# Transposes of normalised tokens and attention output moved from TensorE to DMA, first and last attention unit in two parts, another set of planner constants

## The chip, the cores and the metric

The kernel runs on one core of one Trainium2 chip. The metric is device time in microseconds (us) of one execution; the median of the runs is given. Engines are called PE (TensorE, matmul), DVE (VectorE), ACT (ScalarE), POOL (GpSimd) and SP (SyncE, which here only issues DMAs).

## What is computed

Two transformer layers on one sequence of 2048 tokens with 512 channels, 32 heads of 16 channels each and a gated FFN of width 1792:

```python
def _A_ref(x, wqkv, wo):
    qkv = ...                                  # x @ wqkv, split in q, k, v by head
    scores = jnp.einsum("bhqd,bhkd->bhqk", q, k) * (Dh ** -0.5)
    p = _softmax(scores, axis=-1)
    o = jnp.einsum("bhqk,bhkd->bhqd", p, v)
    return (o as tokens x channels) @ wo
def _B_ref(x, w_gate, w_up, w_down):
    return (_gelu(x @ w_gate) * (x @ w_up)) @ w_down
x = x + _A_ref(_layernorm(x), A_wqkv, A_wo)
x = x + _B_ref(_layernorm(x), B_w_gate, B_w_up, B_w_down)
x = x + _A_ref(_layernorm(x), A_wqkv, A_wo)
x = x + _B_ref(_layernorm(x), B_w_gate, B_w_up, B_w_down)
```

Inputs and output are bfloat16. Both layers use the same weights.

## The kernel before

**Units.** The queries of a layer are cut into blocks (`layer_blocks`: four of 512 tokens in the first layer; three of 512 and two of 256 in the second). A block times a group of four heads is a *unit*; there are 72, and units are worked on in this order. Four heads lie at partitions 0, 32, 64 and 96 of a `QT` or `KT` tile, so that a score matmul uses 32 rows of the PE array.

**Two passes over the scores.** The softmax needs the maximum of a row first. In pass 1 (`p1_emit`) PE makes a 128x512 block of scores, queries on the partitions, in one of PSUM banks 0 to 3 (L1507), and DVE reduces one or two banks to row maxima `PM` (L1522). `fin` reduces the maxima of a unit (L897), transposes them (L899), and four small DMAs on SP put the negated maxima into spare rows of the unit's `QT` slot (`negmax`, L916). In pass 2 (`p2_emit`, `p2_tile`) PE makes the scores again, keys on the partitions, with the maximum subtracted in the same matmul, in banks 4 to 6 (L1378); ACT exponentiates one or two banks to `PT`, a part of the tile `SCR` (L1354); PE multiplies by the values `VP` (L1402) into bank 7, where 17 columns per head hold 16 channels and the row sum. `nrm` takes bank 7 to `ACCS` (L948, ACT), makes the reciprocal of the sums on POOL (L966) and the product on POOL (L971), which goes to `ATT`, tokens on the partitions.

**Folds.** A pair of score blocks can be reduced another way: POOL makes the difference of two key blocks, `KD` (L1149); PE makes scores of the difference (L1327); ACT writes the positive part of them to `SCR` (L1334); DVE adds the other block's scores from PSUM and takes the maximum in one instruction (L1517). This is one ACT instruction more and one DVE reduction less. `want_fold` decides when.

**Around attention.** `ln_to_xnt` normalises tokens (statistics on DVE, the rest on POOL, result `XN`, two slots) and turns each 128x512 tile with `transpose_tile` to `XNT`, channels on the partitions: four PE transposes into a bank (L749) and one eviction on ACT or DVE (L668, L666). From `XNT` come K, Q and V (`kproj`, `qproj`, `vproj`; K and Q go through `SG` and a DMA on SP, L811 and L853, to their head's partitions). `outproj` turns `ATT` in the same manner to `ATTT` (two slots), multiplies by `WO` and adds to the residual `X`. `ffn` normalises `X` again, runs 14 gate GEMMs with GELU on ACT (during which no pass 2 runs, since ACT's table is changed), 14 up GEMMs with the product, and the down GEMM.

**The split.** The first three units of the second layer (`split`, `NSPL=3`) are done in two parts: pass 2 runs over three quarters of the keys with the maximum of those (`fin_part`), the partial result is kept in `ATT` (`keep_part`), and after the last quarter of the keys is there the final maximum is found (`fin_rest`), the last quarter goes through pass 2, and `nrm` scales the kept part by the exponential of the difference of the maxima and adds it.

**The order.** Nothing of the order is decided on the chip. While the program is built, a loop at the end of `_build` keeps an estimated clock for each engine and each tile, and emits at each step the instruction that seems best: a pass 1 matmul, a pass 2 matmul, a piece of a GEMM, or a filler matmul on zeros (L1544) when PE's planned load is low. Work around attention consists of generators (chains) that say what they wait for and carry a due time, counted in pairs of pass 1 matmuls. Moves on SP are emitted when their inputs are estimated to be ready. 19 constants steer the choice; `PLAN` gives a row of them for each 16 pairs of pass 1 (`STRETCH`). They say, among other things, how far pass 2 may fall behind pass 1 (LAG), when evictions go to DVE (LAGT), how late a GEMM piece may make the score matmuls (LIM, OV) and when folds are made (FL, GL, FX). Engines then run their queues in order, with semaphore waits made from the tiles' reads and writes.

The emitted order follows from the estimates alone, for instance those of a DMA on SP, with 0.63 us of queue per issue:

```python
if grp is not None:
    clk[eng] = start + T_DMA * nd
    done = max(clk["dma"], clk[eng] + 1.6) + dur
```

## Time and profile before

| | us |
|---|---|
| median of 3 runs | 2549.27 (2549.22 to 2549.44) |
| the profiled execution, its own time | 2550.05 |
| its span, first to last instruction | 2548.3 |
| POOL busy in the span | 589.6 |
| DMA queue of the program, share of 16 engines | 2.8% |
| granted TensorE clock, mean | 0.999 |

The span is cut by the work in it: up to about 26 us inputs arrive and the first tokens are normalised and projected; up to 80 us pass 1 of the first unit runs beside the projections, and no exponential has run yet; from there to 2493 us pass 1 and pass 2 run side by side, with the output projections, the FFN blocks and (around 1290 to 1400 us) the turn of the layers among them; then the last exponentials follow, and from 2516 us the last block's output projection and FFN.

In the profile a line of a group reads: source line, engine, operation, what it writes and reads, partitions x elements and types, count; busy time in us and mean duration of one in ns; idle time of the engine just before, and what ended it. [...]

### The profile page before, as it was taken

The numbers are of one execution on the slowest core, as the hardware profiler recorded it, in microseconds if no ns is written. First come the engines' busy times: TensorE is split into PE (matmuls) and PEld (weight loads), VectorE is DVE, ScalarE is ACT, GpSimd is POOL, SyncE is SP. The second block draws the span as 40 slices with busy tenths as digits, with TensorE's granted clock in tenths as the row PEclk, the third lists the DMA queues.
The fourth block names the chain that finished last, engine by engine and source line by source line (L and its number), as shares of the span: only waits on it lengthen the run. The fifth ranks groups of instructions, "written<-read, shape, count | busy, mean of one in ns | idle before, by whom it ended". The sixth has DMA issues, their size and how long they took to land.

```text
span 2548.3 us, 67924 instructions
## 1 busy us (share of the span) xinstructions
PE 2450.2 (96%) x29939; PEld 1166.4 (46%) x29939; DVE 2423.5 (95%) x3191; ACT 2356.9 (92%) x3111; POOL 589.6 (23%) x722
## 2 busy tenths in 40 slices
PE   7999999999999999999999999999999999999998
PEld 3444443444434454444434455444543445544555
DVE  7999999999999999999998999999999999999993
ACT  7899998999989999999979899999998999989996
POOL 4010123311133213421133211241113211341200
PEclk9999999999999999999999999999999999999999
DMA  3110000000000000000000000000000000000000
GB/s 100 38 56 6 4 8 2 4 2 2 8 2 4 4 2 6 4 2 16 10 5 4 12 2 4 8 4 8 5 8 1 6 6 3 4 3 12 3 7 6
DMA packets 27367, 25.04 MB, mean 10 GB/s; under 512 B 9408, under 2 KB 26048, under 8 KB 27072
## 3 DMA queue, kind: packets, MB, share of 16 engines
q1 hardware_dynamic: 27072, 20.71, 2.8%
q8 instruction: 234, 3.83, 0.6%
q14 instruction: 61, 0.50, 0.1%
HBM read 9.70 MB, written 2.10 MB: 5 GB/s over the span
## 4 chain that ended last, share of the span: by engine, by line
PE 43%; ACT 32%; DVE 23%; issue 1%; POOL 0%; POOLq 0%; ACTq 0%
ACT SCR L1354 29%; DVE PM L1522 22%; PE PS L1507 14%; PE PS L651 12%; PE PS L1402 9%; PE PS L1378 4%; PE PS L1544 4%; ACT SCR L1334 1%; DVE SCR L1517 1%; PE PS L1327 1%; PE PS L749 0%; ACT XNT L668 0%; ACT SG L668 0%; ACT AO L984 0%; ACT ACCS L948 0%
## 5 line engine op out<-in xcount | busy, mean ns | idle before, releaser
L1522 DVE TENSOR_REDUCE PM<-PS 128x1 f32<-128x512 f32 (+1 forms) x2492 | 2207.6, 948 | 56.2 <-PE PS L1378 27.8
L1354 ACT ACTIVATE SCR<-PS 128x1024 bf16<-128x1024 f32 (+1 forms) x2385 | 2002.7, 931 | 72.4 <-PE PS L1378 51.2
L1507 PE MATMUL PS<-KT,QT 32*128 32x512 bf16 x3914 | 1008.2, 384 | 40.0 <-DVE PM L1522 25.2
L1378 PE MATMUL PS<-QT,KT 32*128 32x512 bf16 (+1 forms) x4608 | 926.3, 360 | 14.0 <-ACT SCR L1354 11.9
L1402 PE MATMUL PS<-VP,SCR 128*128 128x51 bf16 (+1 forms) x16384 | 808.9, 187 | 18.2 <-ACT SCR L1354 13.3
L1402 PEld LDWEIGHTS PS<-VP,SCR 128*128 128x128 bf16 x16384 | 571.0, 96 | 509.7 <-issue 427.1
L1507 PEld LDWEIGHTS PS<-KT,QT 32*128 32x128 bf16 x3914 | 240.8, 91 | 514.7 <-DVE PM L1522 298.2
L1544 PE MATMUL PS<-WV,ZER 128*128 128x240 bf16 x2483 | 432.3, 266 | 4.1 <-ACT SCR L1354 4.1
L966 POOL TENSOR_TENSOR RL<-ACCS,CM 128x16 f32<-128x16 f32 (+1 forms) x63 | 173.4, 2753 | 1032.8 <-ACT ACCS L948 1032.5
L1378 PEld LDWEIGHTS PS<-QT,KT 32*128 32x128 bf16 x4608 | 228.9, 91 | 85.7 <-ACT SCR L1354 62.5
L1544 PEld LDWEIGHTS PS<-WV,ZER 128*128 128x128 bf16 x2483 | 189.0, 96 | 67.9 <-issue 53.9
L1112 POOL TENSOR_TENSOR HT<-HT,AO 128x512 bf16<-128x512 bf16 (+1 forms) x109 | 121.2, 1113 | 273.7 <-ACT AO L1110 273.7
L651 PE MATMUL PS<-WD,HT 128*128 128x512 bf16 x448 | 130.6, 381 | 0.1
L651 PE MATMUL PS<-XNT,WU 128*128 128x512 bf16 (+1 forms) x504 | 127.6, 357 | 0.0
L1517 DVE CUSTOM_DVE_ANT_0 SCR<-PS,SCR 128x512 bf16<-128x512 f32 x182 | 118.0, 685 | 6.0 <-PE PS L1507 2.3
L1149 POOL TENSOR_TENSOR KD<-KT 128x512 bf16<-128x512 bf16 x71 | 81.9, 1154 | 176.1 <-PE PS L1327 162.2
L651 PE MATMUL PS<-XNT,WG 128*128 128x512 bf16 (+1 forms) x504 | 119.4, 359 | 1.3 <-ACT HT L1091 0.9
L1091 ACT ACTIVATE HT<-PS 128x512 bf16<-128x512 f32 (+1 forms) x126 | 69.1, 550 | 50.5 <-PE PS L651 49.5
L1334 ACT ACTIVATE SCR<-PS 128x1024 bf16<-128x1024 f32 (+1 forms) x116 | 99.3, 856 | 16.1 <-PE PS L1327 15.6
L986 POOL TENSOR_TENSOR X<-X,AO 128x512 f32<-128x512 f32 x46 | 58.3, 1268 | 197.2 <-ACT AO L984 197.0
L1110 ACT ACTIVATE AO<-PS 128x512 f32<-128x512 f32 (+1 forms) x109 | 63.8, 585 | 0.4
L651 PEld LDWEIGHTS PS<-XNT,WG 128*128 128x128 bf16 x504 | 39.2, 98 | 53.5 <-issue 29.3
(99 smaller groups left out, 884.9 us busy)
## 6 DMA issues: line engine op xcount, KB each, us to landing
KT<-SG SPq DMA_DIRECT2D x64, 64.0 KB
QT<-MT SPq DMA_DIRECT2D x236, 1.0 KB
QT<-SG SPq DMA_DIRECT2D x56, 64.0 KB
out_dram<-AO SPq DMA_DIRECT2D x16, 128.0 KB, 1.7
WG<-in_B_w_gate_dram SPq DMA_DIRECT2D x4, 448.0 KB, 5.1
WU<-in_B_w_up_dram SPq DMA_DIRECT2D x4, 448.0 KB, 4.8
WD<-in_B_w_down_dram SPq DMA_DIRECT2D x4, 384.0 KB, 4.9
SCR<-in_A_x_dram SPq DMA_DIRECT2D x2, 512.0 KB, 5.4
```

The costliest lines, as they stand in the source:

```text
L651: ins = e.matmul(out_ap, lhsT=l, rhs=r_, start=(i == 0), stop=(i == n - 1))
L966: emit("pool", lambda e: e.tensor_tensor(RL[:, s, 0:4 * nq], lsum, CM1[:, 0:4 * nq], op=ALU.pow), r=[("ACCS", s), ("CM1",)], w=[("RL", s)] ...
L1112: emit("pool", lambda e, ft=ft, o=o: e.tensor_tensor(HT[:, ft, 0:n], HT[:, ft, 0:n], AO[:, o, 0:n], op=ALU.mult), r=[("AO", o), ("HT", ft) ...
L1149: emit("pool", lambda e: e.tensor_tensor(KD[:, s, :], KT[:, g, ka * 512:(ka + 1) * 512], KT[:, g, kb * 512:(kb + 1) * 512], op=ALU.subtrac ...
L1334: emit("act", lambda e: e.activation(PT[:, s0:s0 + cnt, :], PS[:, bk:bk + cnt, :], ACTF.Relu), r=bks, w=[("PT", s0 + d) for d in range(cnt ...
L1354: emit("act", lambda e: e.activation(dst, src, ACTF.Exp, scale=DH ** -0.5), r=[BK[bk + i] for i in range(cnt)], w=[("PT", i) for i in slot ...
L1378: ins = e.matmul(bank(bk)[:, i * n:(i + 1) * n], lhsT=KT[32 * j:32 * j + 32, g, kt * 128:(kt + 1) * 128], rhs=QT[32 * j:32 * j + 32, s, 0: ...
L1402: ins = e.matmul(acc, lhsT=PT[:, slot, i * n + qt * 128:i * n + (qt + 1) * 128], rhs=AP(VP, (kt * H + 4 * g + j) * 17, [[NTT * H * 17, 128 ...
L1507: ins = e.matmul(bank(b), lhsT=QT[32 * j:32 * j + 32, s, qt * 128:(qt + 1) * 128], rhs=KT[32 * j:32 * j + 32, g, kb * 512:(kb + 1) * 512], ...
L1517: emit("dve", lambda e, i=i, b=b, sl=sl: e.tensor_tensor_reduce(PT[:, sl, :], bank(b), PT[:, sl, :], 1.0, -3.0e38, ALU.add, ALU.max, po[:, ...
L1522: emit("dve", lambda e: e.tensor_reduce(po, PS[:, bs[0]:bs[0] + cnt, :], axis=AX.X, op=ALU.max), r=bks, w=[("PM", sm) + h[1:] for h in hs] ...
L1544: return e.matmul(PS[:, b, NACC:512], lhsT=ZER[:, :], rhs=WV[:, 0, 0:512 - NACC], start=(b != 7), stop=(b != 7), skip_group_check=True)
```

## The change

Four things are done at once.

1. **Transposes by DMA.** A new helper `turn_dma` issues four DMA transposes of 128x128 on SP for a tile. It takes the place of `transpose_tile` for normalised tokens (not for the first layer's input, and not for tiles of a group that ends with the last token) and for the attention output (not for the last block of a layer): 64 tiles, 38 of `XNT` and 26 of `ATTT`, 256 DMAs. The PE transposes, 384 before, are 128 after.
2. **First and last unit in two parts.** Unit 0 and unit 71 join the split units, with a second copy of their Q tile on POOL (`q_copy`), since both maxima are needed at once: the first part uses the copy's slot, so the first part's maximum need not be replaced before the second part starts.
3. **The merge of parts** becomes a chain of its own (`merge`), run as soon as both maxima and the kept part are there, in place of four instructions inside `nrm`.
4. **Constants.** All rows of `PLAN` but seven are other ones. V projections of the first layer fall due earlier by 16 (`HV`) for the first three quarters of the keys.

```diff
+        def turn_dma(src_fn, rkeys, dst_fn, wkeys, grp):
+            for ck in range(NCK):
+                wk = [k + (ck,) for k in wkeys]
+                yield ("sp", list(rkeys), wk)
+                emit("sp", lambda e, ck=ck: e.dma_start(dst_fn(ck), src_fn(ck), transpose=True), r=list(rkeys),
+                     w=wk, grp=grp, dur=DTL)
...
-                yield ("pe", [("XN", i % 2)], [("XNT", tt)])
-                transpose_tile(lambda ck, i=i: XN[:, i % 2, ck * 128:(ck + 1) * 128], [("XN", i % 2)],
-                               XNT[:, :, tt * 128:(tt + 1) * 128], [("XNT", tt)])
+                if DT & 1 and tag != ("in", 0) and not (DTX and tts[-1] == NTT - 1):
+                    yield from turn_dma(lambda ck, i=i: XN[:, i % 2, ck * 128:(ck + 1) * 128], [("XN", i % 2)],
+                             lambda ck, tt=tt: XNT[:, ck, tt * 128:(tt + 1) * 128], [("XNT", tt)], "xt%d" % (i % 2))
+                else:
...
+            by_dma = DT & 2 and not (DTX and t0 + n == S)
             def tr(qt):
-                transpose_tile(lambda ck: ATT[:, qt, ck * 128:(ck + 1) * 128], ak, ATTT[:, qt % 2, :, :],
-                               [("ATTT", qt % 2)])
+                if by_dma:
+                    yield from turn_dma(lambda ck: ATT[:, qt, ck * 128:(ck + 1) * 128], ak,
+                             lambda ck: ATTT[:, qt % 2, ck, :], [("ATTT", qt % 2)], "at%d" % (qt % 2))
+                else:
...
+        if HSPL:
+            split[0] = 0
+            n_part[0] = HNA
+            extra[0] = n_qt - 1
+        if TSPL:
+            split[NU - 1] = NSPL
+            n_part[NU - 1] = TNA
+            extra[NU - 1] = NU % n_qt
...
+        def merge(u):
...
+            yield ("cond", lambda: u in kept and u in fin_rec and gel["on"] is None)
+            yield ("pool", [("MSEL", s1), ("MSB", i)], [("DW", i)])
...
+        def q_copy(u):
+            sl, s2 = u % n_qt, extra[u]
...
+            emit("pool", lambda e: e.tensor_copy(QT[:, s2, 0:n], QT[:, sl, 0:n]), r=[("QT", sl)], w=[("QT", s2)], dur=0.05 + n / 710.0)
...
             if FAST and (SF or la == NL - 1) and t0 + n == S and g == NG - 1:
+                src, src_t, src_o, keys = PS, 8 * 512, 7 * 512, [BK[7]]
+                if u in split:
+                    av = ACCS[:, s, 0:na].rearrange("p (a b) -> p a b", a=nq)
+                    emit("dve", lambda e: e.tensor_tensor(av, PS[:, 7, 0:na].rearrange("p (a b) -> p a b", a=nq), pa, op=ALU.add),
+                         r=[BK[7]] + pk, w=[("ACCS", s)], dur=0.1 + 0.067 * nq)
...
-    (0.0, 0.15, 0.45, 0.42, 0.3, -0.05, 1, 1, 62, 84, 8, 60, 0.3, 2.0, 0, 2, 2, 2, 7),
-    (0.1, 0.2, 0.65, 0.42, 0.3, -0.05, 1, 1, 62, 84, 8, 60, 0.3, 2.0, 0, 2, 2, 2, 7),
+    (0.1, 0.15, 0.45, 0.42, 0.3, -0.05, 2, 1, 62, 68, 8, 60, 0.3, 2.0, 5, 2, 2, 2, 7),
+    (0.1, 0.15, 0.45, 0.42, 0.3, -0.05, 2, 1, 62, 68, 8, 60, 0.3, 2.0, 5, 2, 2, 2, 7),
...
```

The columns of a `PLAN` row are SPC, SPLIT, S1C, S2C, OV, LIM, NT, P2B, LAG, LAGT, FL, GL, FX, AHD, DUE, DUEM, PIECE, GP and NPV.

## The prediction

> **What bounds the kernel now.** I read the head of the page first, then the same engines in three windows, then the groups kept apart by shape, then the last 60 us in order of time, and at the end SyncE's queue. Busy time, from the page:

> ```profile
> span 2548.3 us, 67924 instructions
> ...
> PE 2450.2 (96%) x29939; PEld 1166.4 (46%) x29939; DVE 2423.5 (95%) x3191; ACT 2356.9 (92%) x3111; POOL 589.6 (23%) x722
> ```

> PE's 96% is no bound: 2483 of its matmuls are warm-up fillers (L1544). The two engines that read the score banks are: DVE takes the row maximum, ACT the exponential. The windows (columns: width; PE, PEld, DVE, ACT, POOL busy; clock; DMA):

> ```profile
> 0.00:100.00 100.00, 84.75 (x587) 34.89 (x587) 81.19 (x120) 72.77 (x122) 28.25 (x62) 1.00 0.24 69
> 100.00:2450.00 2350.00, 2276.56 (x28139) 1077.83 (x28140) 2287.09 (x2986) 2210.34 (x2895) 558.62 (x654) 1.00 0.03 8
> 2450.00:2548.30 98.30, 88.95 (x1217) 53.69 (x1217) 55.20 (x87) 73.79 (x96) 2.74 (x6) 0.98 0.02 5
> ```

> In the middle DVE is busy 2287.1 of 2350 us, ACT 2210.3: DVE sets the pace, with 62.9 us idle there, 18.8 in the head and 43.1 in the tail (124.8 in all). The groups by shape give the prices:

> ```profile
> L1522 DVE TENSOR_REDUCE PM<-PS 128x2 f32<-128x1024 f32 x1240 | 1493.7, 1217 | 39.7 <-PE PS L1378 19.0 <-PE PS L1507 12.0 <-PE PS L1327 0.4
> L1522 DVE TENSOR_REDUCE PM<-PS 128x1 f32<-128x512 f32 x1252 | 842.9, 682 | 16.5 <-PE PS L1378 8.8 <-PE PS L1507 2.2 <-PE PS L1327 1.7
> L1517 DVE CUSTOM_DVE_ANT_0 SCR<-PS,SCR 128x512 bf16<-128x512 f32 x182 | 118.0, 685 | 6.0 <-PE PS L1507 2.3 <-PE PS L1327 1.8 <-PE PS L1378 1.1
> ...
> L1354 ACT ACTIVATE SCR<-PS 128x1024 bf16<-128x1024 f32 x1711 | 1664.4, 1059 | 63.3 <-PE PS L1378 46.0 <-PE PS L1507 1.9 <-issue 0.2
> L1354 ACT ACTIVATE SCR<-PS 128x512 bf16<-128x512 f32 x674 | 407.6, 606 | 9.1 <-PE PS L1378 5.2
> L1334 ACT ACTIVATE SCR<-PS 128x1024 bf16<-128x1024 f32 x66 | 69.4, 1052 | 6.7 <-PE PS L1327 6.3
> ...
> L668 ACT ACTIVATE XNT<-PS 128x512 bf16<-128x512 bf16 x57 | 34.2, 610 | 10.2 <-PE PS L749 9.9
> ...
> L668 ACT ACTIVATE ATTT<-PS 128x512 bf16<-128x512 bf16 x31 | 18.9, 611 | 1.8 <-PE PS L749 1.7
> ```

> Neighbours' records overlap: the two shapes of L1522 add up to 2336.6 us, while the page gives the line 2207.6 in union over 2492 instructions. So I take 0.05 off each: a double reduction costs 1.15 us (1493.7/1240 less 0.05), a single one 0.62, a fold's DVE part 0.60. ACT's line likewise (2072.1 against 2002.7 over 2385): 0.94 a double exponential, 0.58 a single one. The tail:

> ```profile
> 2493.43 0.21 DVE L897 TENSOR_REDUCE MSEL<-PM 128x8 bf16<-128x32 f32 x1
> 2493.68 0.21 DVE L899 STREAM_TRANSPOSE MT<-MSEL 128x32 bf16<-128x32 bf16 x1
> ...
> 2516.37 0.21 DVE L941 RECIPROCAL RL<-PS 128x8 f32<-128x8 f32 x1 [14.59 <-PE PS L1402]
> ```

> From 2493.8 to 2516.4 DVE has almost nothing to do: ACT still exponentiates. Then 32 us of last block.

> **The change, part by part.** The order of the built program gives the new counts.

> *Work.* DVE: double reductions 1240 to 1321 (81 x 1.15 = +93.2), single ones 1252 to 1170 (-50.8), folds 182 to 142 (40 x 0.60 = -24.0); evictions and gate products nearly cancel (transposes 7 to 3 at 0.41, SG 7 to 4 and VP 5 to 7 at 0.69, products at 0.42 or 0.69: -0.2); the split of two units adds two small maxima, two 32-wide transposes and one addition (+1.2 by L897, L899, L943). Sum **+18.3**. ACT: double exponentials 1711 to 1646 (-61.1), single 674 to 804 (+75.4), fold evictions 66 to 34 doubles at 1.02 and 50 to 74 singles at 0.57 (-19.0), XNT 57 to 23 and ATTT 31 to 5 at 0.58 (-34.8), the rest +0.1: **-39.4**. So ACT is relieved and DVE, which sets the pace, is loaded: fewer folds by the new constants.

> *How much of +18.3 reaches the end.* A fold less helps where ACT is the later engine for the moment. I cut both programs' PE order into stretches of so many score matmuls, priced each stretch's DVE and ACT work by the rows above, and added the larger of the two. Stretches of 128: +16.1 us by the change; of 32: +8.5; of 16: +4.2; of 8: -2.4. Each engine can run ahead by its own banks (four of eight, a few matmuls), so 8 and 32 are the bounds, and I take 16, **+4.2**. The tail is in it: 19 pairs of exponentials follow the last score matmul instead of 23 (4 x 0.94 = -3.8); without that cover the new addition of 0.3 us stands bare.

> *Head.* The first exponential comes after 62 score matmuls instead of 85, but by the 160th both programs have issued 39 pairs. DVE's work up to the 128th is nearly equal (82.4 and 81.0, in the sum already). DVE idles 7 us between 26 and 80 us; bounds -7 and 0, I take **-1**.

> *PE.* 256 of 384 transposes go: their records (25.6 and 12.4 us for 256 and 128) say 0.10 us each, 25 us in all, but fillers rise from 2483 to 2643: PE is being kept busy. Only 60 of the 384 stand in stretches that have no fillers, so -6 to 0, taken as nothing.

> *The transposes' new way.* 64 tiles x 4 = 256 DMAs on SP's queue, none of which the trace shows. The nearest rows are plain moves between SBUF tiles:

> ```profile
> 1303.75 1.17 SPq L811 DMA_DIRECT2D KT<-SG  x2
> 1313.61 2.34 SPq L916 DMA_DIRECT2D QT<-MT  x4
> ```

> 0.585 us to issue one, so 2.34 a tile and 150 us more of a queue that now issues 543 times; the output stores land 1.7 us after issue, the slowest row (an HT load) 8.0. A tile thus takes 2.34 - 0.59 + 1.7 = 3.5 us at best, 10 by the slowest row. What it may take: PE is in order, and the output projection that waits for a block's first tile stands at least 8.0 us of DVE work behind the last PV matmul that the tile needs; ACT's eviction (0.42), POOL's power (2.91) and product (0.62) take 4.0 of that. Room 4.0 against 3.5: covered, barely. The FFN's first gate matmul has 8.3 us or more, less 1.8 for POOL. Without cover a late tile stops PE, and both readers run dry within about a bank. Queued behind on SP are the max moves (L916, 300) and the Q and K moves; a max move gets up to 2.3 us later, which matters only where ACT has no older unit left, and there are few. I take half a microsecond at each of seven blocks, **+3**; bounds 0 and 60 (rival 1).

> [...]

> **Sum.** 2548.3 + 4.2 - 1 + 3 = 2554.5 of span. The median of the runs (2549.27) is 1.0 above the profiled span (that execution itself took 2550.05), so **2555.5 us**.

> **Rivals.** (1) *Transposes late.* If one DMA transpose holds the queue twice as long as a plain move, 1.2 us, a tile takes 4 x 1.2 + 1.1 = 5.9 instead of 3.5, 1.9 over the room at the first tile of seven blocks (13), and 1.7 over at each of 19 later tiles, whose uses stand some 3.1 us apart (32). About half is absorbed by work already in the banks: 20 to 45, **2580**. It decides once a tile passes 4.0 us. For it: nothing in the trace shows a fast one. Against: plain moves of all sizes issue alike.
> (2) *Faster.* DVE's 62.9 idle us in the middle end mostly in PE matmuls (L1378 27.8, L1507 14.2). With fewer evictions between scores and with the new order the fine cut (-2.4) holds, the filler-free stretches get their 6 back, the head its 7: 2548.3 - 15.4 + 1 = **2534**. It decides if PE, and not DVE, ends the waits. Against: DVE has more to do in every coarse cut.
> (3) *All of DVE's work counts.* ACT is nowhere the later engine: +18.3 - 3.8, and transposes are hidden: **2564**.
> (4) *The splits do nothing*: head and tail as before, +4.2 + 3.8 + 3: within the forecast's range at 2560.

> **Chances.** Forecast with (4), 2547 to 2562: 0.42; rival 1: 0.18; rival 2: 0.26; rival 3: 0.14. 0.2% (5 us) is about what a measurement tells from none. Faster than 2544: rival 2 and a little, 0.29. Within 5 us: the forecast's lower half, 0.22. Slower: 0.49. Range: 2533 to 2583, from rival 2 to just past rival 1; the forecast's own 2547 to 2562.

> **What would show it.** DVE's busy time near 2442 and ACT's near 2317, with DVE's idle time in the middle near 60; SP's transposes issuing in about 0.6 us; PE's wait for ATTT or XNT DMAs under 10 us in all; 2493.8 to the end shortened by some 4 us. Wrong if PE waits for transposes for tens of us (rival 1), or if DVE's idle time falls under 95 (rival 2).

## The result, and the profile after

The changed kernel takes 2692.39 us (median of 4 runs, 2689.26 to 2695.57) beside 2549.36 us for the kernel before, measured beside it: a ratio of 1.0557, 95% interval 1.0544 to 1.0570, 143 us slower. The profiled execution took 2689.26 us; its span is 2687.5. Of all executions in this document one is slow, over 1.5% above the quickest of its kernel: the profiled one of e7 below, which that run's time and ratio leave out.

The head of the page after:

```profile
span 2687.5 us, 67730 instructions
...
PE 2501.6 (93%) x29639; PEld 1174.5 (44%) x29843; DVE 2448.5 (91%) x3112; ACT 2338.1 (87%) x3111; POOL 588.2 (22%) x719
...
PEclk9999999999889998999999999899988999999899
```

DVE's and ACT's busy times are within 7 and 21 us of what was predicted (2442 and 2317). The 139 us that the span grew are mostly idle time: DVE idles 239.0 us instead of 124.8, ACT 349 instead of 191. And the row of PE's granted clock, whose mean was 0.999 before, now has dips: the mean is 0.969.

The windows after, with the two ends cut where the same work begins and ends, and two of 100 us around FFN blocks (columns as before: width; PE, PEld, DVE, ACT, POOL busy; clock; DMA):

```profile
0.00:100.00 100.00, 84.23 (x538) 33.62 (x544) 76.41 (x118) 73.02 (x131) 29.00 (x64) 0.95 0.23 68
100.00:2590.00 2490.00, 2329.31 (x27951) 1088.03 (x28141) 2315.40 (x2905) 2194.68 (x2886) 555.90 (x647) 0.97 0.04 10
2590.00:2687.50 97.50, 88.10 (x1157) 52.80 (x1161) 56.72 (x91) 70.38 (x96) 3.31 (x8) 0.98 0.02 6
700.00:800.00 100.00, 92.79 (x742) 33.75 (x751) 80.80 (x116) 71.79 (x106) 26.57 (x49) 0.81 0.04 9
2000.00:2100.00 100.00, 91.23 (x741) 34.10 (x752) 78.08 (x108) 70.35 (x102) 26.67 (x44) 0.80 0.05 10
```

The first of the two stretches in the kernel before:

```profile
700.00:800.00 100.00, 96.16 (x1006) 40.33 (x1002) 97.78 (x146) 93.02 (x140) 36.88 (x61) 1.00 0.01 2
```

The loss is in the middle, where DVE now idles 174.6 us instead of 62.9, and in pieces: the two windows at FFN blocks hold 41 us of DVE idle time between them, and there the clock is 0.81 and 0.80. What ends the waits (waiter, line, what it waited for: us in all, times, longest), before:

```profile
ACT SCR L1354 <- PE PS L1378: 51.2, 149, 3.6
...
DVE PM L1522 <- PE PS L1378: 27.8, 90, 2.7
```

and after:

```profile
ACT SCR L1447 <- PE PS L1471: 122.6, 226, 8.4
...
DVE PM L1616 <- PE PS L1471: 75.7, 138, 5.7
...
PE PS L673 <- DMA XNT<-XN: 31.7, 5, 7.9
...
PE PS L673 <- DMA ATTT<-ATT: 29.3, 14, 5.0
```

The readers wait for PE's scores, and PE for transposes. The lines of the transposes alone, from the view of one source line (count, shortest, median and longest issue in ns; then who waited; then issue to landing in us):

```profile
L781 SPq DMA_TRANSPOSE XNT<-XN x152: 1093/1233/2424, 393.2 to 2529.8; - x152
L781 SPq DMA_TRANSPOSE ATTT<-ATT x104: 1093/1233/2272, 370.9 to 2508.1; - x104
...
  PE PS L673: 61.1, 19
  PEld PS L673: 32.9, 10
...
DMA to landing us min/median/max: 2.2/2.4/4.3
```

The max moves in the same view before:

```profile
L916 SPq DMA_DIRECT2D QT<-MT x300: 520/521/689, 75.6 to 2495.6; - x150
```

One DMA transpose holds SP's queue 1.233 us, where the max move's issue took 0.521 us. So a tile of four takes about 3 x 1.27 + 2.37 = 6.2 us from its first issue to its last landing, instead of the 3.5 of the prediction. The chain that ended last shows one such tile at 697 us (start, us, what):

```profile
697.40 1.16 SPq L781
698.61 1.23 SPq L781
699.88 1.24 SPq L781
701.16 2.38 DMA ATTT<-ATT
703.67 0.59 PE PS L673 x2
```

And tiles queue behind each other. SP's queue in order of time around it:

```profile
689.63 5.29 SPq L781 DMA_TRANSPOSE ATTT<-ATT  x4
...
697.40 10.09 SPq L781 DMA_TRANSPOSE ATTT<-ATT  x8
709.47 18.76 SPq L781 DMA_TRANSPOSE XNT<-XN  x14
728.27 2.28 SPq L985 DMA_DIRECT2D QT<-MT  x4
730.60 2.38 SPq L781 DMA_TRANSPOSE XNT<-XN  x2
```

The FFN's first gate matmul needs four `XNT` tiles, 16 transposes or 20 us of queue. By SP's place in the order the last two even stand behind a max move. PE, in order, meanwhile (in brackets: the idle time before, and what ended it):

```profile
703.67 0.59 PE L673 MATMUL PS<-WO,ATTT 128*128 128x512 bf16 x2 [3.04 <-DMA ATTT<-ATT]
704.20 0.39 PE L1601 MATMUL PS<-KT,QT 32*128 32x512 bf16 x2
...
704.97 0.60 PE L1601 MATMUL PS<-KT,QT 32*128 32x512 bf16 x1
...
734.56 0.39 PE L1601 MATMUL PS<-KT,QT 32*128 32x512 bf16 x2 [1.77 <-DMA XNT<-XN]
...
735.20 0.60 PE L1601 MATMUL PS<-KT,QT 32*128 32x512 bf16 x2
```

Two things happen. PE stops, 3.04 and 1.77 us here. And soon after each stop the same score matmul lasts 0.60 instead of 0.39 us: the granted clock has gone to half. Summed over the trace, PE stops 63.5 us ahead of the 34 matmuls that wait for a transpose (from each one's weight load; the longest 7.6 us). By the trace's clock records the clock is at half for 169.2 us in 17 pieces, against 5.9 us before; these records hold no clock but full and half. One more stop of 3.3 us, at 408 us, is not among the 34: it waits for a max move that stands behind ten transposes on SP.

### The profile page after: what moved, and what is told of

Its sections match the earlier page's. It is cut to its first block, busy times and chain, and to the rows that moved or that the text cites. A ratio compares the mean times of both kernels' runs of the same rounds, so it can differ in the third digit from the quotient of the medians.

```text
span 2687.5 us, 67730 instructions
## 1 busy us (share of the span) xinstructions
PE 2501.6 (93%) x29639; PEld 1174.5 (44%) x29843; DVE 2448.5 (91%) x3112; ACT 2338.1 (87%) x3111; POOL 588.2 (22%) x719
## 4 chain that ended last, share of the span: by engine, by line
PE 47%; DVE 30%; ACT 14%; SPq 5%; issue 2%; DMA 2%; POOL 1%; POOLq 0%; ACTq 0%
DVE PM L1616 28%; PE PS L1601 15%; ACT SCR L1447 13%; PE PS L673 12%; PE PS L1495 10%; PE PS L1638 5%; PE PS L1471 4%; SPq L781 4%; DMA ATTT<-ATT 1%; DVE SCR L1611 1%; DMA XNT<-XN 1%; PE PS L1420 0%; SPq L985 0%; POOL RL L1041 0%; PE PS L771 0%
## 5 line engine op out<-in xcount | busy, mean ns | idle before, releaser
L1616 DVE TENSOR_REDUCE PM<-PS 128x2 f32<-128x1024 f32 (+1 forms) x2491 | 2257.3, 967 | 161.1 <-PE PS L1471 75.7
L1447 ACT ACTIVATE SCR<-PS 128x1024 bf16<-128x1024 f32 (+1 forms) x2450 | 2017.3, 909 | 147.5 <-PE PS L1471 122.6
L1471 PE MATMUL PS<-QT,KT 32*128 32x512 bf16 (+1 forms) x4608 | 958.7, 364 | 21.5 <-ACT SCR L1447 15.0
L1638 PE MATMUL PS<-WV,ZER 128*128 128x240 bf16 x2643 | 468.6, 268 | 5.5 <-ACT SCR L1447 4.7
L1638 PEld LDWEIGHTS PS<-WV,ZER 128*128 128x128 bf16 x2643 | 203.6, 97 | 82.8 <-issue 64.0
L673 PE MATMUL PS<-XNT,WG 128*128 128x512 bf16 (+1 forms) x487 | 132.2, 395 | 33.6 <-DMA XNT<-XN 31.7
L673 PE MATMUL PS<-WD,HT 128*128 128x512 bf16 x384 | 116.6, 380 | 6.3 <-issue 3.7
L1427 ACT ACTIVATE SCR<-PS 128x512 bf16<-128x512 f32 (+1 forms) x108 | 80.1, 742 | 48.1 <-PE PS L1420 47.9
L1611 DVE CUSTOM_DVE_ANT_0 SCR<-PS,SCR 128x512 bf16<-128x512 f32 x142 | 90.8, 686 | 19.0 <-PE PS L1601 15.9
L673 PE MATMUL PS<-WO,ATTT 128*128 128x512 bf16 x105 | 41.4, 467 | 30.8 <-DMA ATTT<-ATT 29.3
```

The lines of the kernel that those rows point to most:

```text
L673: ins = e.matmul(out_ap, lhsT=l, rhs=r_, start=(i == 0), stop=(i == n - 1))
L1447: emit("act", lambda e: e.activation(dst, src, ACTF.Exp, scale=DH ** -0.5), r=[BK[bk + i] for i in range(cnt)], w=[("PT", i) for i in slot ...
L1471: ins = e.matmul(bank(bk)[:, i * n:(i + 1) * n], lhsT=KT[32 * j:32 * j + 32, g, kt * 128:(kt + 1) * 128], rhs=QT[32 * j:32 * j + 32, s, 0: ...
L1611: emit("dve", lambda e, i=i, b=b, sl=sl: e.tensor_tensor_reduce(PT[:, sl, :], bank(b), PT[:, sl, :], 1.0, -3.0e38, ALU.add, ALU.max, po[:, ...
L1616: emit("dve", lambda e: e.tensor_reduce(po, PS[:, bs[0]:bs[0] + cnt, :], axis=AX.X, op=ALU.max), r=bks, w=[("PM", sm) + h[1:] for h in hs] ...
L1638: return e.matmul(PS[:, b, NACC:512], lhsT=ZER[:, :], rhs=WV[:, 0, 0:512 - NACC], start=(b != 7), stop=(b != 7), skip_group_check=True)
```

## Experiments

Fourteen kernels ran, each timed in three rounds beside the kernel before. Ratios are to that kernel. "Stops" are PE's idle time ahead of matmuls that wait for a transpose's DMA, "half clock" the time at half the granted clock, both from the profiled execution. That one has the least half clock of its four in e1 and the most in e13 and e14. The merge as a chain stays in all fourteen.

| | us | ratio (95%) | stops | half clock |
|---|---|---|---|---|
| changed kernel | 2692.39 | 1.0557 (1.0544 to 1.0570) | 63.5 | 169.2 |
| e1 PE transposes | 2553.02 | 1.0005 (0.9991 to 1.0020) | 0 | 0.4 |
| e4 only the DMA transposes | 2662.71 | 1.0442 (1.0427 to 1.0457) | 64.5 | 130 |
| e3 only `XNT` by DMA | 2641.42 | 1.0365 (1.0348 to 1.0383) | 48.6 | 95.6 |
| e11 only the constants | 2558.42 | 1.0029 (1.0018 to 1.0041) | 0 | 10.2 |
| e12 only the splits | 2568.07 | 1.0071 (1.0056 to 1.0086) | 0 | 17.1 |
| e6 one DMA a tile | 2575.91 | 1.0100 (1.0085 to 1.0114) | 3 | 6.1 |
| e5 four DMAs, planned at cost | 2616.03 | 1.0257 (1.0242 to 1.0272) | 8.4 | 17 |
| e9 one DMA, planned at cost | 2559.93 | 1.0038 (1.0023 to 1.0053) | 1.9 | 0 |
| e10 as e9, constants and units of before | 2578.19 | 1.0111 (1.0096 to 1.0126) | 11 | 18 |
| e13 order of the changed kernel, one DMA | 2573.88 | 1.0092 (1.0074 to 1.0109) | 1.6 | 23.9 |
| e7 625 fillers in the stops | 2674.95 | 1.0498 (1.0453 to 1.0543) | 20.9 | 142.7 |
| e8 1057 fillers in the stops | 2692.60 | 1.0561 (1.0544 to 1.0579) | 0.9 | 23 |
| e14 e13 with 633 fillers | 2641.28 | 1.0343 (1.0317 to 1.0370) | 0 | 38.2 |
| e15 e13 with 1057 fillers | 2679.86 | 1.0505 (1.0481 to 1.0530) | 0 | 3.4 |

### Which part of the change

PE transposes in the changed kernel, all else kept (e1):

```diff
-DT=3
+DT=0
```

> The changed kernel with all 64 tiles turned on PE again; splits and constants stay. Theory A (the DMA transposes arrive later than the planned order allows, PE stops for them and its clock is halved afterwards): within 15 us of the kernel before, 2535 to 2565, half clock under 15 us. Rival B (the new constants and splits suit the kernel badly): above 2640, with DVE and ACT idle as in the changed kernel.

No loss is left: 1.0005. The splits and the constants together are worth nothing that can be told, and the whole loss comes with the DMA transposes. The other way round, the DMA transposes alone with the constants and units of before (e4):

```diff
-HSPL=1, TSPL=1
+HSPL=0, TSPL=0
-PLAN = [...]   # the changed kernel's rows
+PLAN = [...]   # the rows of before
```

> The kernel before with nothing but the transposes moved to DMA: its own constants, no new splits. Theory A: slower than before by 80 to 200 us, with PE waiting some 60 us on the transposes. Rival B: within 20 us of before (2530 to 2570).

2662.71 us, 1.0442: four fifths of the loss, with as many stops, 64.5 us. Constants alone (e11: `DT=0`, `HSPL=0, TSPL=0`) and splits alone (e12: `DT=0`, the rows of before):

> The new constants alone, with PE transposes and without the two new splits. If the constants were made for the order with splits: 2560 to 2600, and with the splits they give before's time; if splits and constants are each neutral: 2545 to 2560.

> The two new splits alone, with PE transposes and the constants of the kernel before. If splits help where the constants fit and the old ones do not fit them: 2560 to 2590. If neutral: 2545 to 2560; faster than 2545 would say that the new constants hide a gain of the splits.

Both are a little slower than before, 1.0029 and 1.0071, while together they cost nothing that can be told. e11 lies in its range for "neutral", e12 above it, so the splits seem to need the new constants; part of both excesses is half clock (10.2 and 17.1 us). Last, DMA transposes for `XNT` alone, PE transposes for `ATTT` (e3):

```diff
-DT=3
+DT=1
```

> The changed kernel with the 38 tiles of normalised tokens by DMA (four a tile) and the 26 tiles of attention output on PE. PE waited 32 us for the former and 29 us for the latter, so about half of the loss should stay: 2600 to 2640, with some 30 us of waits on XNT. If both share one queue and make each other late, less: under 2590.

1.0365, about two thirds of the loss with 152 of the 256 transposes, just above the 2640 us that were expected, with more waits than the expected 30 us. Seven stops at the gate GEMMs bear it, up to 10.7 us long.

### What a transpose costs

One DMA transpose of 128x512 for a tile instead of four of 128x128, planned as the four were, at 2.52 us of queue (e6):

```diff
-            for ck in range(NCK):
-                wk = [k + (ck,) for k in wkeys]
-                yield ("sp", list(rkeys), wk)
-                emit("sp", lambda e, ck=ck: e.dma_start(dst_fn(ck), src_fn(ck), transpose=True), r=list(rkeys),
-                     w=wk, grp=grp, dur=DTL)
+            yield ("sp", list(rkeys), list(wkeys))
+            emit("sp", lambda e: e.dma_start(dst, src, transpose=True), r=list(rkeys),
+                 w=list(wkeys), grp=grp, dur=DTL, hold=2.52)
```

> The changed kernel with one DMA transpose of 128x512 for a tile instead of four of 128x128; the planner books the same 2.52 us of queue. If a transpose costs by the instruction (1.3 us of issue each), a tile lands about 3.7 us after its issue begins, PE's waits on transposes fall from 63 us to under 10, and the time is 2540 to 2570. If it costs by the data, the one issue holds the queue about 5.3 us, a tile lands 7.5 us after its issue begins, and the time stays within 30 us of 2692.

The same view of its transposes as above:

```profile
L779 SPq DMA_TRANSPOSE XNT<-XN x38: 1188/1191/2119, 381.4 to 2412.6; - x38
L779 SPq DMA_TRANSPOSE ATTT<-ATT x26: 1189/1226/1842, 366.1 to 2395.4; - x26
...
DMA to landing us min/median/max: 2.3/2.4/4.1
```

The price is per instruction: 128x512 holds the queue 1.19 us (`XNT`) or 1.23 us (`ATTT`) where 128x128 held it 1.233 us, and both land 2.4 us after their issue. Nobody waits for it for long, and 118 of the 143 us are gone; the time is still 6 us above the 2570 that were expected.

Four DMAs again, but with the planner told what they cost (e5):

```diff
-                     w=wk, grp=grp, dur=DTL)
+                     w=wk, grp=grp, dur=0.0, hold=1.27, lat=1.14)
```

> The changed kernel, still with four DMA transposes a tile, but the planner is told what the trace shows: 1.27 us of queue each and landing 1.14 us after the issue's end (it believed 0.63 and 1.9). Theory A (the order places the readers of a tile too early): PE's waits on transposes under 10 us, half clock under 20 us, time 2555 to 2600. Rival C (the queue is simply overloaded by 326 us of transposes, wherever the readers stand): above 2630.

2616.03 us lies between the two theories' numbers. The stops are nearly gone (8.4 us), so the wrong estimate made them; but the kernel is still 65 us slower than before. Its stops and its 17 us of half clock (at 0.4 us each, see below) make some 15 of that; the rest, about 50 us, lies in an order that leaves 20 us of queue ahead of each gate. In its waits ACT stands 78.0 us for score matmuls and DVE 29.7 us, in four waits, for evictions to `ACCS` (L1031); which choice of the planner causes that was not followed up.

One DMA with its true price (e9: as e6, `hold=1.25, lat=1.2`), and the same with the constants and units of before (e10):

> One DMA transpose for a tile, and the planner is told its measured cost, 1.25 us of queue and landing 1.2 us later. If the 25 us that the one-DMA kernel is slower than with PE transposes came from the planner booking 4.4 us a tile: 2545 to 2560. If they come from constants that were made for another order, or from the DMA way itself: 2565 to 2585 again.

> The kernel before, its own constants and no new splits, with one DMA transpose for a tile at its true cost in the planner. If the DMA way is no worse than PE once it arrives in time: 2535 to 2560, and if relief of ACT (35 us of evictions) counts, the lower half. If the constants' fit to an order is what is lost: 2565 to 2585.

e9 comes within 0.4% of before, e10 does not. So 16 of e6's 25 us went with the planner's wrong price, and e10's time falls into the range that was expected if the constants no longer fit the order. No version is faster than before; e1 alone has it within its interval.

### How lateness turns into 143 us

The changed kernel's order on PE, DVE, ACT and POOL, instruction by instruction, but the first of a tile's four DMAs carries the whole tile, and the other three are not issued (e13):

```diff
-                emit("sp", lambda e, ck=ck: e.dma_start(dst_fn(ck), src_fn(ck), transpose=True), r=list(rkeys),
-                     w=wk, grp=grp, dur=DTL)
+                emit("sp", (lambda e: e.dma_start(dst, src, transpose=True)) if ck == 0 else (lambda e: []), r=list(rkeys),
+                     w=wk, grp=grp, nd=int(ck == 0), dur=DTL, hold=T_DMA)
```

> The changed kernel with the very same order of instructions on PE, DVE, ACT and POOL; only SP differs: a tile's first DMA transpose carries all four blocks and the other three are not issued. Theory A, lateness alone: waits on transposes under 8 us, half clock under 15 us, and 2545 to 2565; that would make lateness 130 to 147 of the 143 us. If part of the loss lies in the new order itself: above 2575.

```profile
ACT SCR L1447 <- PE PS L1471: 75.5, 201, 4.5
...
DVE PM L1616 <- PE PS L1471: 29.4, 107, 0.9
```

Its waits, beside those of the changed kernel: ACT's are down by 47 us, DVE's by 46. The time is 2573.88 us. Lateness and all that follows from it is worth 1.0557 - 1.0092, 118 us; about 24 us remain without it, more than the 2545 to 2565 us that were expected for the order alone.

But 63.5 us of stops are not 118. Two attempts to keep the clock up by putting warm-up fillers, 0.1 us each, into the stops (e7 with 625, and e8 with 1057):

```diff
         sch.plan()
+        late = [o for o in sch.streams["pe"] if any(e[:2] in ("xt", "at") for e, _ in o.waits)]
+        for o, n in zip(late, STALL):
+            at = sch.streams["pe"].index(o)
+            sch.streams["pe"][at:at] = [_Op("pe", -1, fill) for _ in range(n)]
```

> The changed kernel with filler matmuls (0.1 us each, on zeros, into unused columns of bank 7) put ahead of each matmul that was seen to wait for a transpose, as many as fill that wait, so that PE is late but not idle. If the halved clock after the waits is a cost of its own: half clock falls from 169 us to under 60 us and the time by 40 to 75 us, to 2617 to 2652. If only the waits cost: within 15 us of 2692.

> The changed kernel with 106 us of filler matmuls spread over all 34 waits for transposes, more than the waits themselves (63 us), so that PE should nowhere stand still there. If the halved clock costs about 0.4 us for each us of it: half clock under 30 us and a time of 2650 to 2680, no slower than the 2684 of the scanter filling in spite of twice the fillers. If the clock costs nothing and PE's lateness alone does (140 us lost for 63 us of waits, a factor of 2.2): above 2740.

In e7 other stops remained, and its other three executions lie 28 us apart, so its median tells little (what their spread tells follows below). In e8 the half clock is mostly gone, and the time is that of the changed kernel, in neither of the expected ranges; but it holds PE up by 106 us where the stops were 63.5, so a missing half clock and an added delay may have cancelled. The two had to be parted in the kernel in which nothing is late: e13 with the same diff, 63.3 us of fillers as long as the measured stops, place by place (e14), and with e8's 105.7 us (e15):

> The kernel with the changed kernel's order and every transpose in time (2573.88 us), with 633 warm-up fillers of 0.1 us ahead of the 34 matmuls that waited for a transpose in the changed kernel: at each as many as fill the stop measured there (63.5 us in all). PE is as late at each place as there, but never stands still, so the clock should stay full. Theory A (the half clock has a price of its own): a late us costs 1.0 to 1.2 us, 2637 to 2650 us, and the 42 to 55 us that are missing to 2692 are the price of 146 us at half clock. Theory B (lateness alone, 118 us for 63.5, the clock costs nothing): 2685 to 2700 us with hardly any half clock. If half clock is there all the same, fillers do not keep the clock, and the run tells nothing of A and B.

> The same with 1057 fillers (106 us), as many as in the overfilled changed kernel, in the kernel whose transposes come in time. Theory A: 2680 to 2700 us, like the overfilled kernel, since a late us costs 1.0 to 1.2. Theory B: 118 us for each 63.5 late, 2765 to 2775 us. If the price of a late us grows with the length of a stop, the step from 63 to 106 us of fillers costs more than the first 63 in proportion; if it shrinks, the readers' banks cover a fixed part of each stop.

By the medians e14 adds 67.4 us for 63.3 us of fillers, e15 106.0 for 105.7. But some half clock is left in these runs (38.2 us in e14's profiled execution), and not the same in each execution. The record has the mean granted clock of every execution, to 0.001; 0.001 less is some 5 us at half clock:

| | us (mean granted clock) |
|---|---|
| e13 | 2569.39 (0.999), 2569.80 (0.999), 2577.95 (0.995), 2577.96 (0.995) |
| e14 | 2634.22 (0.999), 2638.92 (0.997), 2643.63 (0.995), 2648.24 (0.993) |
| e15 | 2676.26 (0.999), 2676.28 (0.999), 2683.45 (0.997), 2685.07 (0.996) |
| e7 | 2664.90 (0.995), 2674.95 (0.990), 2693.10 (0.981) |
| e8 | 2685.65 (0.996), 2690.71 (0.994), 2694.49 (0.992), 2695.36 (0.992) |
| changed kernel | 2689.26 (0.969), 2690.30 (0.968), 2694.49 (0.965), 2695.57 (0.965) |

Three things can be read from it.

- *A late us costs 1 us.* At 0.999, e14 takes 64.6 us more than e13 for 63.3 us of fillers, e15 106.7 for 105.7. So PE's lateness costs what it lasts, with no absorption, and not twice that.
- *Half clock has a price of its own.* Executions of one program run the same instructions in the same order, and the time goes with the clock: 14.0 us for some 32 us of half clock in e14, 8.4 for 21 in e13, 28.2 for 76 in e7, which is 0.37 to 0.44 us per us. (The smaller spreads of e15, e8 and the changed kernel give 0.5, 0.4 and 0.3; there the rounding of the clock weighs more.)
- *The many transposes cost nothing else.* At 0.996, e8 with its 256 transposes takes 2685.65 us and e15 with 64 takes 2685.07, with the same fillers.

From e14 at 0.999 to the changed kernel's profiled execution, equally late at the same places, there remain 55 us, and about 164 us more of half clock. 26 of them fall into the stops, where PE has nothing to run; for the other 138 that is 0.40 us each, or 0.37 if the 3.3 us stop for the max move, which e14 does not have, is taken off first.

Another measure of the half clock fell out of two profiles. Up to 365 us e1 and e13 have the same order on PE. Both stop at the same place for 1.32 us; only e13's clock then goes to half, for 10.2 us. PE in e1:

```profile
54.50 0.39 PE L1601 MATMUL PS<-KT,QT 32*128 32x512 bf16 x2 [1.32 <-DVE PM L1616]
...
55.95 0.38 PE L771 MATMUL PS<-IDN,XN 128*128 128x128 bf16 x4
```

and in e13:

```profile
54.59 0.39 PE L1601 MATMUL PS<-KT,QT 32*128 32x512 bf16 x2 [1.32 <-DVE PM L1616]
...
56.06 0.59 PE L771 MATMUL PS<-IDN,XN 128*128 128x128 bf16 x4
```

The same max move is then issued on SP, in e1 and in e13, at

```profile
354.88 2.25 SPq L985 DMA_DIRECT2D QT<-MT  x4
```

```profile
359.30 2.25 SPq L985 DMA_DIRECT2D QT<-MT  x4
```

4.42 us later, 0.09 of it there before: 4.3 us for 10.2 us of half clock, 0.42 per us, before any DMA transpose is issued.

So of 143 us about 65 are PE's lateness, about 58 what else comes with late transposes (2692.39 - 2634.22), nearly all of it the half clock, and about 20 are the order: e13 at 0.999 beside the kernel before.

## Why the prediction was wrong

**The step that failed** is the price of a transpose: "0.585 us to issue one, so 2.34 a tile". It took a plain move's row for an operation that the trace did not show. A transpose took 1.233 us, a tile 6.2 us instead of 3.5, against a room of 4.0. The threshold of 4.0 fits the runs (tiles that land 2.4 us after their issue, e6, stop PE for 3 us, these for 63.5), and the term "half a microsecond at each of seven blocks, +3" became 118 us. Both ends of its bound, 0 and 60, were too low.

**Rival 1** had the mechanism: 1.2 us of queue, 5.9 a tile, PE stopped. Its size, 20 to 45 us, failed in three places. It counted each tile's own excess over its room, where 16 transposes of an FFN block queue up for 20 us, so that stops were 63.5 and not 45 us. It let "about half" be absorbed by the banks; e14 and e15 show that nothing is. And it had no half clock: it foresaw stops of 1.7 and 1.9 us, and here the clock was half for 20.5 us after a stop of 1.77 us; the half clock brought nearly all of another 58 us. The 1.2 us stood there as twice a plain move's issue, which no trace had shown for a transpose; the trace after has 1.233 us of queue, and 2.4 from issue to landing. The prediction gave this rival 0.18.

**DVE's and ACT's work.** DVE's was counted rightly, 2442 us against 2448.5 after and 2444.4 in e13, though its terms add up to +19.4 and not to the +18.3 that stands there. ACT's instructions were too, but their busy time fell by 19 to 23 us (2338.1 and 2334.1) and not by 39.4; why was not followed up. What of DVE's work reaches the end, +4.2 by the cut at 16 score matmuls, was too little if e13's 20 us are all DVE's work (it is busy 20.9 us longer there than before, and rival 3 let all of it count); that this is the reason was not tried.

**Splits and constants** near nothing: right (e1). The tail shrinks: from the last maxima's transpose (L966, 2497.20 us) to the end e1 takes 48.7 us, before 54.6, so 5.9 where 3.8 was predicted. The head shows no gain: in the first 100 us DVE is busy 80.61 us in e1 and 81.19 before, and in the changed kernel 76.41, with the half clock at 56 us between it and e1.

**PE's 25 us of transposes taken as nothing**: right. e9 takes them off PE, with 1.9 us of stops and no half clock, and is no faster (2559.93 us) than e1, which keeps them (2553.02). So the move had little to win: it freed an engine that had 2483 fillers to spare, and loaded a queue for which PE, in order, has to wait.

## What to carry to other kernels

A new kind of DMA is priced by one look at itself, not by the row of another kind (here 1.233 us of queue, and 0.521 for the max move); its price here is per instruction (1.19 to 1.23 us for 128x512, 1.233 for 128x128), so one large transpose stands for four. Where an order is made from estimates, an optimistic one puts an in-order engine's consumers ahead of their data (PE stopped 63.5 us here, and 8.4 once the planner had the measured price), and the queue's total per block (20 us here), not a single tile's latency (6.2), is to be held against the room. A stop on PE is here priced at its full length (64.6 us for 63.3), and the half clock comes on top (0.37 to 0.44 us for each us of it). And where executions of one program differ, their clocks beside their times are an experiment that costs no run.
